# Six token blocks through the weights a quarter at a time, a weight conversion without GpSimd, a mask on ScalarE, and issue in the written order

## The chip, the cores and the metric

The kernel runs on one core of a Trainium2 chip. The metric is the device time of one execution in microseconds. Times are medians of several runs where several were made; "span" is the same execution in the trace, some 1.8 us shorter. "Cold" and "warm" are used of TensorE by the length of its matmuls: the same twelve h matmuls take 2.75 to 2.86 us when warm and up to 4.5 when cold.

## The reference, cut to what matters

```python
# r, k, v: (4 batches, 8 heads, 768 steps, 48 channels), f32
for t in range(S):
    cur = einsum('bhd,bhe->bhde', u * k[:, :, t], v[:, :, t])
    y[:, :, t] = einsum('bhd,bhde->bhe', r[:, :, t], state + cur)
    state = w * state + einsum('bhd,bhe->bhde', k[:, :, t], v[:, :, t])
x = y.transpose(0, 2, 1, 3).reshape(3072, 384)
h = x @ w_in                # 384 x 2048
g = h - tanh(h)
out = g @ w_out             # 2048 x 384
```

Two kinds of work: the recurrence, done in "units" of 64 steps and two batches (24 units), and the dense part, done in 12 blocks of 256 tokens with 8 dense steps each (96 steps). Two units make the input of one block. The weights arrive as 64-bit numbers and are turned into f32 on the chip.

## The kernel before

Engine names in the code: T is TensorE, V VectorE, A ScalarE, G GpSimd. A dense step is 12 h matmuls, then elementwise work on ScalarE, GpSimd and VectorE that makes g, and the output matmuls two steps later:

```python
        def first(f):
            h = ps_d.tile([128, 2, d.NT], F32, name="h", tag="h")
            ...                                    # 12 matmuls
            A.activation(s, hf, AF.Square)
            A.activation(th, hf, AF.Tanh)
            A.activation(q1, s, AF.Square, bias=m1b)
            A.activation(q2, s, AF.Square, bias=m2b)
            G.tensor_scalar(small, s, SMALL, None, ALU.is_lt)
            V.scalar_tensor_tensor(cube, s, C4, hf, ALU.mult, ALU.mult)
            V.tensor_tensor(gf, hf, th, ALU.subtract)
            V.scalar_tensor_tensor(cube, q1, K1, cube, ALU.add, ALU.mult)
            V.scalar_tensor_tensor(cube, q2, K2, cube, ALU.add, ALU.mult)
            V.copy_predicated(gf, small.bitcast(I32), cube)
            return g
```

A unit is one long chain through all engines:

```python
        G.tensor_tensor(kw[:, :, :D], kt, w_down, ALU.mult)
        ...
        for src in (rt, kw):
            for p in range(NP):
                T.transpose(turned[...], src[...], ident)
            if src is rt:
                V.tensor_tensor(halves(rT), turned, halves(w_up), ALU.mult)
            else:
                A.copy(halves(kT), turned)
        G.tensor_tensor(rk, rt[:, :, :D], kt, ALU.mult)
        G.tensor_tensor(rk, rk, ub, ALU.mult)
        yield
        V.tensor_reduce(du, rk, axis=mybir.AxisListType.X, op=ALU.add)
        G.tensor_tensor(at, same[...], du[...], ALU.mult)
        ...                                        # state x rT; rT x kT into lev
        yield
        V.copy_predicated(at, before, lev)
        yield
        ...                                        # at x vt; vt x kw: the "value groups"
        A.copy(xt[...], y_ps[...]); A.copy(rest, ...)
        yield
        V.tensor_tensor(now, kv_ps, now, ALU.add)  # the state
        G.tensor_tensor(now, now, w_all, ALU.mult)
        yield
```

In words: rT and kT are r and k turned round, kw is k times its decay, du is the share of the step itself, and `at` is first a mask (`same` times du: one GpSimd operation here, in the changed kernel's early units eight on ScalarE), into which the predicated copy then puts the product of rT and kT. The "value groups" use `at`. Note that `turned` is one buffer: the kw transposes may go only after rT has read the rt transposes. Units and dense steps are generators, and `weave` writes them into the program in turns. All 28 weight pieces are converted in the first two blocks' units, ahead of the first dense step. The framework's scheduler then chooses the order of the instructions on each engine; only the small matmuls are held to the written order:

```python
    def put(*args, **how):
        tc.keep_in_program_order(T.matmul(*args, skip_group_check=True, **how))
```

## Time and profile before

| | before |
|---|---|
| time, median of 4 runs | 728.44 us (726.28 to 729.8) |
| TensorE busy | 620.9 us, 86% |
| VectorE / ScalarE / GpSimd busy | 492.4 / 279.5 / 352.6 us |
| granted TensorE clock, mean | 0.946 |
| TensorE's time before 182 us beyond its work at the warm pace | 114.5 us, worked out in the prediction |
| of it without any matmul, by the trace's busy time | 93.1 us (182 less 88.9) |

Its lines stand in the prediction. Read them as one story: TensorE is full from a quarter of the way on, and the only time to win lies in the front, where the weights are converted.

### The profile page before, as it was taken

The numbers are of one execution on the slowest core, as the hardware profiler recorded it, in microseconds if no ns is written. First come the engines' busy times: TensorE is split into PE (matmuls) and PEld (weight loads), VectorE is DVE, ScalarE is ACT, GpSimd is POOL, SyncE is SP. The second block draws the span as 40 slices with busy tenths as digits, with TensorE's granted clock in tenths as the row PEclk, the third lists the DMA queues.
The fourth block names the chain that finished last, engine by engine and source line by source line (L and its number), as shares of the span: only waits on it lengthen the run. The fifth ranks groups of instructions, "written<-read, shape, count | busy, mean of one in ns | idle before, by whom it ended". The sixth has DMA issues, their size and how long they took to land.

```text
span 724.0 us, 13305 instructions
## 1 busy us (share of the span) xinstructions
PE 620.9 (86%) x5060; PEld 453.2 (63%) x5060; DVE 492.4 (68%) x739; ACT 279.5 (39%) x510; POOL 352.6 (49%) x289
## 2 busy tenths in 40 slices
PE   1462473657999999999999999999999999999996
PEld 0351452435776777777677777767777777777773
DVE  7764788989875664864865766748648656576563
ACT  1110413223443543444444434435435444354442
POOL 4775876758654543634545445436345243133231
PEclk9997586767999999999999999999999999999999
DMA  9457243422210211202102102112120010000001
GB/s 145 99 127 138 68 101 90 108 80 74 51 36 11 55 29 41 41 15 58 26 13 58 36 10 58 30 31 42 24 47 15 1 27 3 4 23 1 23 1 27
DMA packets 89722, 33.80 MB, mean 47 GB/s; under 512 B 80561, under 2 KB 86066, under 8 KB 89650
## 3 DMA queue, kind: packets, MB, share of 16 engines
q1 hardware_dynamic: 85042, 20.28, 14.9%
q10 hardware_dynamic: 4608, 12.59, 6.3%
q8 instruction: 42, 0.69, 0.4%
q14 instruction: 30, 0.25, 0.1%
HBM read 26.94 MB, written 4.72 MB: 44 GB/s over the span
## 4 chain that ended last, share of the span: by engine, by line
PE 68%; DVE 12%; DMA 8%; POOL 6%; issue 4%; SPq 1%; ACT 0%; ACTq 0%; DVEq 0%; POOLq 0%
PE o L177 33%; PE h L151 27%; PE yk_ps L348 4%; DMA st<-in_moe_w_out_dram 4%; DMA rt<-in_r_dram 3%; POOL part L119 3%; PE x_ps L363 2%; POOL rk L370 2%; POOL rk L371 2%; DVE st L116 1%; DVE part L114 1%; DVE w_in_sb L117 1%; DVE part L118 1%; DVE w_in_sb L115 1%; DVE cube L170 1%
## 5 line engine op out<-in xcount | busy, mean ns | idle before, releaser
L151 PE MATMUL h<-xt,w_in_sb 128*128 128x256 f32 x1152 | 276.4, 389 | 20.6 <-POOL w_in_sb L120 20.5
L177 PE MATMUL o<-w_out_sb,g 128*128 128x384 f32 x768 | 270.0, 498 | 11.8 <-DVE g L171 11.8
L166 POOL TENSOR_SCALAR small<-s 128x512 f32<-128x512 f32 x96 | 146.1, 1523 | 258.0 <-ACT s L162 249.7
L151 PEld LDWEIGHTS h<-xt,w_in_sb 128*128 128x128 f32 x1152 | 217.1, 194 | 59.8 <-POOL w_in_sb L120 22.9
L177 PEld LDWEIGHTS o<-w_out_sb,g 128*128 128x128 f32 x768 | 146.8, 194 | 102.4 <-issue 11.6
L167 DVE SCALAR_TENSOR_TENSOR cube<-s,h 128x512 f32<-128x512 f32 x96 | 65.7, 685 | 122.6 <-ACT th L163 122.4
L162 ACT ACTIVATE s<-h 128x512 f32<-128x512 f32 x96 | 57.3, 597 | 190.7 <-PE h L151 87.1
L170 DVE SCALAR_TENSOR_TENSOR cube<-q,cube 128x512 f32<-128x512 f32 x96 | 79.2, 825 | 7.6
L171 DVE COPY_PREDICATED g<-small,cube 128x512 f32<-128x512 int32 x96 | 78.5, 818 | 5.6
L169 DVE SCALAR_TENSOR_TENSOR cube<-q,cube 128x512 f32<-128x512 f32 x96 | 74.8, 779 | 0.0
L164 ACT ACTIVATE q<-s,m1b 128x512 f32<-128x512 f32 x96 | 69.3, 722 | 9.9 <-POOL part L119 9.9
L165 ACT ACTIVATE q<-s,m2b 128x512 f32<-128x512 f32 x96 | 69.0, 719 | 0.0
L168 DVE TENSOR_TENSOR g<-h,th 128x512 f32<-128x512 f32 x96 | 65.5, 682 | 0.0
L163 ACT ACTIVATE th<-h 128x512 f32<-128x512 f32 x96 | 56.8, 592 | 2.7 <-POOL part L119 2.7
L119 POOL TENSOR_TENSOR part<-part,st 128x384 f32<-128x384 f32 (+1 forms) x28 | 35.9, 1280 | 39.6 <-DVE part L118 22.8
L348 PE MATMUL yk_ps<-rT,state 48*64 48x64 f32 x704 | 27.7, 234 | 24.3 <-DVE state L416 19.3
L113 ACT ACTIVATE st<-st 128x384 f32<-128x384 uint32 (+1 forms) x28 | 17.1, 610 | 73.3 <-POOL part L119 34.5
L348 PEld LDWEIGHTS yk_ps<-rT,state 48*64 48x64 f32 x704 | 24.6, 146 | 33.1 <-issue 28.2
L376 POOL TENSOR_TENSOR at<-same,du 128x512 f32<-128x512 f32 x24 | 30.9, 1286 | 23.9 <-PE yk_ps L348 21.4
L365 DVE TENSOR_TENSOR rT<-x_ps,w_up 128x512 f32<-128x512 f32 x24 | 16.4, 685 | 29.3 <-PE x_ps L363 29.3
L374 DVE TENSOR_REDUCE du<-rk 128x8 f32<-128x384 f32 x24 | 13.2, 550 | 33.3 <-POOL rk L371 33.3
L370 POOL TENSOR_TENSOR rk<-rt,kt 128x384 f32<-128x384 f32 x24 | 26.6, 1109 | 16.5 <-DMA rt<-in_r_dram 9.5
(71 smaller groups left out, 459.8 us busy)
## 6 DMA issues: line engine op xcount, KB each, us to landing
st<-in_moe_w_out_dram ACTq DMA_DIRECT2D x16, 384.0 KB, 3.0
st<-in_moe_w_in_dram ACTq DMA_DIRECT2D x24, 192.0 KB, 3.3
rt<-in_r_dram SPq DMA_DIRECT2D x48, 96.0 KB, 3.1
kt<-in_k_dram SPq DMA_DIRECT2D x48, 96.0 KB, 3.0
vt<-in_v_dram SPq DMA_DIRECT2D x48, 96.0 KB, 2.8
out_dram<-o SPq DMA_DIRECT2D x48, 96.0 KB, 2.2
xt<-rest SPq DMA_DIRECT2D x144, 8.0 KB, 1.8
st<-in_moe_w_in_dram ACTq DMA_DIRECT2D x24, 64.0 KB, 3.3
```

The costliest lines, as they stand in the source:

```text
L119: G.tensor_tensor(part_f, part_f, lo_f, ALU.mult)
L151: T.matmul(h[:, z], w_in_sb[:, kk, (f + z) * 128 : (f + z + 1) * 128], xt[:, kk].rearrange("p b t -> p (b t)"), start=kk == 0, stop=kk == ...
L164: A.activation(q1, s, AF.Square, bias=m1b)
L165: A.activation(q2, s, AF.Square, bias=m2b)
L166: G.tensor_scalar(small, s, SMALL, None, ALU.is_lt)
L167: V.scalar_tensor_tensor(cube, s, C4, hf, ALU.mult, ALU.mult)
L168: V.tensor_tensor(gf, hf, th, ALU.subtract)
L169: V.scalar_tensor_tensor(cube, q1, K1, cube, ALU.add, ALU.mult)
L170: V.scalar_tensor_tensor(cube, q2, K2, cube, ALU.add, ALU.mult)
L171: V.copy_predicated(gf, small.bitcast(I32), cube)
L177: T.matmul(outs[i], g[:, z, i * C : (i + 1) * C], w_out_sb[:, f + z, :], start=f + z == 0, stop=f + z == d.NF - 1)
L348: tc.keep_in_program_order(T.matmul(*args, skip_group_check=True, **how))
```

## The change

Its intent is to fill that front. The weights come in eight pieces of 1536 columns; six blocks run their first quarter of the dense part as soon as the first quarter of the weights is there, then all six their second, and so on, with partial sums in SBUF. The conversion uses VectorE and ScalarE only, the mask `small` goes from GpSimd to ScalarE, early units use VectorE and ScalarE instead of GpSimd, and the scheduler is switched off, so that each engine issues in the written order. The diff, cut to its core:

```diff
-            G.tensor_tensor(part_f, part_f, lo_f, ALU.mult)
-            G.tensor_tensor(dst, dst, part_f, ALU.add)
...
+        V.tensor_scalar(power, hi, 0x7FF00000, None, ALU.bitwise_and)
+        A.activation(power, power, AF.Relu, scale=8.0, bias=self.bias)
+        V.tensor_scalar(bits, hi, 0xFFFFF, 0x100000, ALU.bitwise_and, ALU.bitwise_or)
+        A.activation(lo_f, lo, AF.Copy, scale=2.0**-52)
+        yield
+        V.scalar_tensor_tensor(dst, bits, 2.0**-20, lo_f, ALU.mult, ALU.add)
+        V.scalar_tensor_tensor(power, hi, 0x80000000, power, ALU.bitwise_and, ALU.bitwise_or)
+        yield
+        V.tensor_tensor(dst, dst, power.bitcast(F32), ALU.mult)
...
-            G.tensor_scalar(small, s, SMALL, None, ALU.is_lt)
+        A.activation(small, s, AF.Relu, bias=smallb, scale=-1.0)
...
+            if begun:
+                V.tensor_tensor(o, outs[i], o, ALU.add)      # partial sums
...
+        weave(blocks([0, 1]), pieces([0, 1]))
+        for q in range(4):
+            fs = (q * part, (q + 1) * part)
+            streams = [(chain.from_iterable(dense(j, xts[j], fs) for j in js), FIRST * part // 2)]
+            if q == 0:
+                streams.append(blocks(range(2, FIRST + 2)))
+            if q < 3:
+                streams.append(pieces([2 * q + 2, 2 * q + 3]))
+            weave(*streams)
...
+        early = n < L * (FIRST + 2)
+        E = V if early else G
+        E.tensor_tensor(kw[:, :, :D], kt, w_down, ALU.mult)
...
+        for h in range(H if early else 0):
+            A.mul(at[:, h % 2, h // 2], same, du[:, h : h + 1])
...
-        tc.keep_in_program_order(T.matmul(*args, skip_group_check=True, **how))
+        T.matmul(*args, skip_group_check=True, **how)
...
-        near(tc, r, k, v, w, u, out, shared, weights)
+        with tc.manual_schedule():
+            near(tc, r, k, v, w, u, out, shared, weights)
```

## The prediction

> **What bounds the kernel now.** I read the page first (busy shares, slices), then the table of stretches, then the costliest groups, then the timeline of one undisturbed step.
>
> ```profile
> span 724.0 us, 13305 instructions
> ...
> PE 620.9 (86%) x5060; PEld 453.2 (63%) x5060; DVE 492.4 (68%) x739; ACT 279.5 (39%) x510; POOL 352.6 (49%) x289
> ...
> PE   1462473657999999999999999999999999999996
> ...
> DVE  7764788989875664864865766748648656576563
> ...
> PEclk9997586767999999999999999999999999999999
> ```
>
> TensorE is full from slice 11 on. Before that it is half idle, and VectorE is busiest.
>
> ```profile
> 0.00:45.00 45.00, 13.71 (x220) 10.49 (x220) 33.67 (x60) 8.15 (x15) 31.13 (x43) 1.00 0.67 121
> 45.00:90.00 45.00, 19.89 (x298) 16.99 (x299) 26.87 (x46) 8.96 (x17) 31.46 (x28) 0.70 0.49 107
> ...
> 135.00:182.00 47.00, 26.42 (x197) 17.29 (x196) 42.42 (x61) 12.65 (x23) 33.03 (x26) 0.75 0.33 89
> ...
> 232.00:282.00 50.00, 49.39 (x433) 36.22 (x432) 32.66 (x48) 21.86 (x40) 23.14 (x19) 1.00 0.17 35
> ...
> 633.00:675.00 42.00, 41.95 (x162) 30.42 (x161) 26.44 (x40) 19.69 (x35) 12.29 (x8) 1.00 0.04 10
> ```
>
> The columns are the stretch, its length, then busy time of PE, PEld, DVE, ACT, POOL, granted clock, DMA share, GB/s. In the chain of waits the blocks stand 50.3 us apart from 182 us on while two attention units run beside each (nine blocks), and 41.7 us apart for the last two: TensorE alone sets the pace. So a unit costs TensorE (50.3 - 41.7) / 2 = 4.3 us, and all its work is 12 x 41.7 + 24 x 4.3 = 604 us. The other 120 us are idle: 7 after the last matmul, and 182 - (41.7 + 6 x 4.3) = 114.5 before 182 us, where the conversion of the weights passes 28 pieces through two staging buffers. That front is what the change attacks.
>
> ```profile
> L151 PE MATMUL h<-xt,w_in_sb 128*128 128x256 f32 x1152 | 276.4, 389 | 20.6 <-POOL w_in_sb L120 20.5
> ...
> L164 ACT ACTIVATE q<-s,m1b 128x512 f32<-128x512 f32 x96 | 69.3, 722 | 9.9 <-POOL part L119 9.9
> ```
>
> The matmuls that wait, wait for the conversion's last GpSimd step. The dense step I use as a ruler:
>
> ```profile
> 644.12 2.75 PE L151 MATMUL h<-xt,w_in_sb 128*128 128x256 f32 x12
> ...
> 646.97 0.60 ACT L162 ACTIVATE s<-h 128x512 f32<-128x512 f32 x1 [2.93 <-issue]
> 647.46 0.59 ACT L163 ACTIVATE th<-h 128x512 f32<-128x512 f32 x1
> ...
> 648.08 0.69 DVE L167 SCALAR_TENSOR_TENSOR cube<-s,h 128x512 f32<-128x512 f32 x1 [0.44 <-ACT th L163]
> 648.69 0.68 DVE L168 TENSOR_TENSOR g<-h,th 128x512 f32<-128x512 f32 x1
> ...
> 649.29 0.68 DVE L169 SCALAR_TENSOR_TENSOR cube<-q,cube 128x512 f32<-128x512 f32 x1
> ...
> 650.07 0.69 DVE L170 SCALAR_TENSOR_TENSOR cube<-q,cube 128x512 f32<-128x512 f32 x1
> ...
> 650.87 0.75 DVE L171 COPY_PREDICATED g<-small,cube 128x512 f32<-128x512 int32 x1
> ```
>
> TensorE goes on 2.6 us after it started h; VectorE starts 1.4 us after that and needs 3.5 us: g is ready about 5 us after h.
>
> **What the Trainium skill says.** "TensorE: Matmul & The Clock Gate", section "Architectural detail": ScalarE and VectorE are strict FIFO, and TensorE pulls only weight loads ahead. No trace line of before contradicts it; it means that a written order is an executed order, and a blocked instruction holds all behind it. The same page, Part 1: an idle window of about 3.4 us halves the clock until a busy one has passed. The trace agrees: after an idle 6.4 us at 144.9 four output matmuls took 2.90 us, against 2.74 for eight when warm. "ScalarE: Activation LUTs", "What ACT_TABLE_LOAD costs": an activation takes 186 ns + 0.833 ns an element, 93 more for each pointer operand, and neighbours overlap by 93. For 512 elements with one pointer that is 706 ns; the trace has 722. "GPSIMD Engine Reference", table of specifications: its SBUF port is shared with VectorE's two-input and two-port operations. The trace agrees: the conversion's fused two-input step took 1.37 to 1.65 us beside GpSimd (107.1, 112.0) and 0.69 alone (108.9).
>
> **The change, part by part.**
>
> Conversion. Uncontended, VectorE's one-input step takes 0.34 us for 384 columns and 0.43 for 512, the fused one 0.55 and 0.69, ScalarE's 0.56 and 0.67. Extended to 1536 columns: 1.15, 1.8 and 1.55 us. A new piece is 2 x 1.15 + 2 x 1.8 + 1.7 = 7.6 us on VectorE and 3.1 on ScalarE; eight are 61 and 25 us, against 98.9 of VectorE and 68.7 of GpSimd before. Real, and mostly hidden after the first quarter.
>
> Start: four units with two pieces, no dense work. The decay table is ready near 12 us as before. One unit in written order is kw, rT, transposes, kT, rk twice, du, eight ScalarE masks, predicated copy, two matmul groups, state: about 8 us, plus 15 us of conversion of which half stands on the path: 12 + 32 + 8 = 52 us, of which TensorE works 17.
>
> First quarter: twelve dense steps with twelve units. The instruction order shows exactly one unit between two h groups, and on VectorE the next unit's kw behind the dense chain. So every step is one loop, us by start-to-start: matmul end to VectorE start 1.4; five dense operations 3.6 (one more dependent pair than before); state 0.45, kw 0.4, rT 0.6, rk 0.5 and 0.6, du 0.6 (rows of 384 and 512 elements: 0.54, 0.685, 0.55); eight masks on ScalarE, with one pointer 0.24 each by the page, 1.9; wait and predicated copy 0.8; attention value groups 1.1 (64 matmuls at 227.9); h 2.6. Sum 14.6. The transposes and kT lie beside rk and du. Two pieces add 15 us in twelve steps, so 15.9 a step, 191 us; some cold stretches, say 4: 195 us. TensorE has only 12 x (5.2 + 4.3) = 114 us of work there.
>
> Quarters two to four: 18 blocks' quarters of two dense steps. TensorE wants 10.4 us each. But the single-buffered sums are now emptied by two VectorE adds behind the second dense chain, 5.0 + 0.9 after h, while TensorE returns after 5.2: 0.7 lost each. With conversion bursts: 18 x 11.4 = 205 us, against 187.
>
> Steady blocks, four left with units. Written order puts rT behind the dense chain and the state add, ready about 6.1 us after h; GpSimd's state multiply (0.89) and then kw (1.0 to 1.35) come behind that, 7.5 us. TensorE stands at the kw transposes 3.1 us after h (2.6 of output matmuls, 0.45 of rt transposes) and waits 4.4. Before, the scheduler put h matmuls there. First and last units about 3: 6 x 4.4 + 2 x 3 = 32 us, and idle over 3.4 us makes the next matmuls cold, 5: 4 x 50.3 + 37 = 238 us.
>
> Last two blocks 83, tail 7. The mask on ScalarE frees 146 us of GpSimd but is not on the path: ScalarE goes to 2.9 us a step of 5.2.
>
> Sum: 52 + 195 + 205 + 238 + 83 + 7 = 780 us.
>
> **Rivals.** (a) The intended one: quarters fill the front. Then only TensorE's work counts: 604 + 35 idle at the start + 7 = 646, perhaps 670 with small waits. For it: the front's 114 us of idle are real. Against it: one unit per dense step in a fixed order is a loop of 14.6 us whatever the engines' load is. (b) Front cured no further than now, but no stalls in the steady blocks: 52 + 190 + 195 + 201 + 90 = 728, the same. For it: the steady state is at 1.00 clock and full; against it: the in-order wait for rT and kw is in the order itself. (c) The clock falls in the first quarter as it did from 45 to 182 us (0.70 to 0.75): h, value groups and transposes stretch, 2 us more a step, 805 us. (d) VectorE becomes the bound in the middle quarters: 3.6 + 0.45 + 1.3 = 5.3 us a step against 5.2: no more than a few us.
>
> **Range and chances.** I take 775, a little under the sum because waits that I counted apart may cover one another. With every term at its kindest (45, 180, 192, 222, 90) it is 729; with (c) and 12 us more elsewhere 815. Range 730 to 812. Faster by over 2% needs a first quarter under some 150 us or no stalls at all: 0.12. Same: 0.14. Slower: 0.74.
>
> **What would show it.** In the changed profile: dense steps about 15 to 16 us apart in the first quarter, with TensorE near 60% busy there and the clock below 1; VectorE's h-to-g chain and the masks inside the loop; pairs of 10.4 to 11.5 us in the middle; blocks of about 59 us with units, waits of 3 to 5 us at the kw transposes released by GpSimd's kw or VectorE's rT; GpSimd near 15% busy. It is wrong if steps in the first quarter come 11 us apart or closer, if the middle runs above 12 us a pair, or if the steady blocks stay at 50 us.

## The result, and the profile after

| | before | after |
|---|---|---|
| time, median | 728.44 us (726.28 to 729.8, 4 runs) | 859.54 us (856.49 to 863.83, 4 runs) |
| ratio | | 1.181 (1.1745 to 1.1869) |
| TensorE busy | 620.9 us | 665.7 us |
| granted clock, mean | 0.946 | 0.899 |

A ratio is the mean time of one kernel's runs over the mean of the other's of the same rounds, so not quite the ratio of the medians. The change makes the kernel 131 us slower, where the prediction said 47. The page of the profile, in the same rows as before:

```profile
span 862.1 us, 12870 instructions
...
PE 665.7 (77%) x5062; PEld 495.3 (57%) x5062; DVE 495.5 (57%) x721; ACT 374.4 (43%) x722; POOL 64.8 (8%) x73
...
PE   0444657656645698989889998897797798899996
...
PEclk9999767686667789999999999999999999999999
```

TensorE is at 0.7 or less up to slice 14 (302 us), where before it was so up to slice 10 (181 us), and its clock is at 0.6 to 0.8 for eleven slices, where before had seven of 0.5 to 0.8. Behind that it no longer holds 9s. The table of stretches, cut at the borders of the change's parts (columns as in the prediction):

```profile
0.00:80.00 80.00, 25.39 (x484) 20.86 (x484) 35.35 (x59) 20.40 (x50) 8.40 (x23) 1.00 0.61 111
80.00:311.00 231.00, 145.94 (x1853) 117.55 (x1854) 99.92 (x150) 79.76 (x201) 16.70 (x12) 0.70 0.25 47
311.00:523.00 212.00, 195.34 (x721) 137.77 (x721) 170.95 (x234) 117.57 (x193) 5.93 (x4) 0.98 0.13 30
523.00:762.00 239.00, 205.61 (x1652) 151.66 (x1650) 127.97 (x192) 104.12 (x188) 33.76 (x35) 0.95 0.13 25
```

These are the start, the first quarter, quarters two to four, and the four blocks with units. In the first quarter no engine is near full: TensorE 63%, VectorE 43%, ScalarE 35%, GpSimd 7%. That is the sign of a loop of dependent instructions, not of a full engine. The waits view (who waits on whom, us in total, times and the longest) names the largest wait of TensorE, of which twelve waits and 60.0 us lie in the first quarter:

```profile
PE x_ps L414 <- DVE rT L416: 85.4, 18, 11.1
```

TensorE stands at the kw transposes until VectorE has made rT, and in the written order rT comes behind the whole elementwise chain of the step.

A step of the first quarter with no conversion in it, cut to the lines of the loop:

```profile
127.66 4.52 PE L165 MATMUL h<-xt,w_in_sb 128*128 128x256 f32 x12
...
133.33 0.69 DVE L182 TENSOR_TENSOR g<-h,th 128x512 f32<-128x512 f32 x1 [7.61 <-ACT th L178]
...
137.06 0.55 DVE L473 TENSOR_TENSOR state<-yk_ps,state 128x384 f32<-128x384 f32 x1
...
140.40 2.02 ACT L428 ACTIVATE at<-same,du 128x64 f32<-128x64 f32 x8
...
143.52 1.13 PE L396 MATMUL yk_ps<-at,vt 64*64 64x64 f32 x32 [0.93 <-DVE at L444]
144.43 1.05 PE L396 MATMUL yk_ps<-vt,kw 64*64 64x48 f32 x32
145.41 0.93 PEld L165 LDWEIGHTS h<-xt,w_in_sb 128*128 128x128 f32 x3
```

The prediction's links in their order: h, the dense chain on VectorE, the state, eight masks on ScalarE, the value groups, the next h 17.75 us after the last. The h group takes 4.52 us here, and took 2.75 in the ruler of before. The start holds two rows of weight loads that the prediction has no counterpart for:

```profile
0.80 17.16 ACTq L125 DMA_DIRECT2D st<-in_moe_w_in_dram  x8
...
21.59 0.56 DVE L410 TENSOR_TENSOR kw<-kt,w_down 128x384 f32<-128x384 f32 x1 [8.21 <-ACT w_down L339]
...
23.53 1.12 PE L414 MATMUL x_ps<-ident,kw 128*128 128x128 f32 x4 [0.78 <-DVE rT L416]
...
52.19 10.05 ACTq L125 DMA_DIRECT2D st<-in_moe_w_in_dram  x7
...
62.28 1.57 ACT L142 ACTIVATE power<-power,p_bias 128x1536 uint32<-128x1536 uint32 x1 [9.93 <-DMA st<-in_moe_w_in_dram]
...
65.91 0.56 DVE L473 TENSOR_TENSOR state<-yk_ps,state 128x384 f32<-128x384 f32 x1 [10.80 <-ACT rest L463]
```

ACTq is ScalarE's own sequencer. A row takes several issues together: a single one takes 0.3 to 0.5 us, but the eight lie over 17.16 us and the seven over 10.05, with gaps of up to 6 us between them; what holds the sequencer in the gaps the trace does not name. Until the last is out ScalarE's next instruction, written behind them, stands; behind it stand the copies that a unit needs, and behind those VectorE's state. One trap for the reader: the granted clock is given as 1.00 for the first 80 us, yet the kw transposes at 23.53 took 1.12 us, as long as the cold ones in the first quarter (1.11 at 138.72), where warm ones take 0.66 (e12, below). Judge the clock by the length of a known group.

In the blocks with units the prediction's wait is there to the digit, in the first line of these two from the waits view:

```profile
PE x_ps L414 <- POOL kw L410: 26.4, 6, 4.4
...
PE o L195 <- DVE part L203: 17.0, 17, 3.1
```

The second line is TensorE waiting for the sums to be emptied, nearly all of it in quarters two to four (16.7 us in 16); the prediction had 0.7 us eighteen times. The first wait in time order, with the cold h group that follows it:

```profile
559.82 0.99 POOL L410 TENSOR_TENSOR kw<-kt,w_down 128x384 f32<-128x384 f32 x1
560.87 0.91 PE L414 MATMUL x_ps<-ident,kw 128*128 128x128 f32 x4 [4.40 <-POOL kw L410]
561.57 4.23 PE L165 MATMUL h<-xt,w_in_sb 128*128 128x256 f32 x12
```

### The profile page after: what moved, and what is told of

Its sections match the earlier page's. It is cut to its first block, busy times and chain, and to the rows that moved or that the text cites. A ratio compares the mean times of both kernels' runs of the same rounds, so it can differ in the third digit from the quotient of the medians.

```text
span 862.1 us, 12870 instructions
## 1 busy us (share of the span) xinstructions
PE 665.7 (77%) x5062; PEld 495.3 (57%) x5062; DVE 495.5 (57%) x721; ACT 374.4 (43%) x722; POOL 64.8 (8%) x73
## 4 chain that ended last, share of the span: by engine, by line
PE 55%; DVE 23%; ACT 8%; issue 6%; DMA 4%; SPq 1%; POOL 1%; DVEq 0%; ACTq 0%; POOLq 0%
PE h L165 25%; PE o L195 18%; PE yk_ps L396 7%; DVE th L185 3%; DVE th L184 3%; DVE g L182 3%; DVE th L183 3%; PE x_ps L414 3%; ACT s L177 2%; DVE g L186 2%; ACT th L178 2%; PE x_ps L396 2%; DMA vt<-in_v_dram 2%; ACT st L144 1%; DVE part L203 1%
## 5 line engine op out<-in xcount | busy, mean ns | idle before, releaser
L165 PEld LDWEIGHTS h<-xt,w_in_sb 128*128 128x128 f32 x1152 | 234.2, 206 | 49.9 <-issue 0.8
L414 PE MATMUL x_ps<-ident,kw 128*128 128x128 f32 x96 | 24.6, 406 | 111.8 <-DVE rT L416 85.4
L186 DVE COPY_PREDICATED g<-small,th 128x512 f32<-128x512 int32 x96 | 71.7, 747 | 10.6 <-DVE th L185 0.9
L185 DVE SCALAR_TENSOR_TENSOR th<-q,th 128x512 f32<-128x512 f32 x96 | 67.0, 698 | 10.3 <-DVE th L184 0.5
L184 DVE SCALAR_TENSOR_TENSOR th<-q,th 128x512 f32<-128x512 f32 x96 | 66.7, 695 | 10.0
L181 ACT ACTIVATE small<-s,smallb 128x512 f32<-128x512 f32 x96 | 68.8, 716 | 0.0
L183 DVE SCALAR_TENSOR_TENSOR th<-s,h 128x512 f32<-128x512 f32 x96 | 65.9, 687 | 3.3
L476 POOL TENSOR_TENSOR state<-state,power 128x384 f32<-128x384 f32 x22 | 29.6, 1347 | 395.8 <-DVE state L473 355.0
L444 DVE COPY_PREDICATED at<-before,x_ps 128x512 f32<-128x512 int32 x24 | 17.3, 721 | 48.5 <-ACT at L428 24.4
L396 PE MATMUL yk_ps<-at,vt 64*64 64x64 f32 x768 | 23.7, 286 | 25.1 <-DVE at L444 18.6
L396 PEld LDWEIGHTS yk_ps<-at,vt 64*64 64x64 f32 x768 | 19.6, 190 | 32.4 <-DVE at L444 21.3
```

The source lines that it names most:

```text
L165: T.matmul(h[:, z], w_in_sb[:, kk, (f + z) * 128 : (f + z + 1) * 128], xt[:, kk].rearrange("p b t -> p (b t)"), start=kk == 0, stop=kk == ...
```

## The experiments

I cut every trace at the same five places, the start of the tanh in dense steps 1, 12, 48, 80 and 96, read from ScalarE's timeline. The stretches add to the span. In e5 and e11 the tanh is written one step later, which moves their cuts by some us. The expectations cut one step later, at 13, 49 and 81, which gives 221, 219 and 236 us for the changed kernel's quarter, middle and blocks with units. The traced run of the changed kernel was the longest of its four (863.83 us), so differences of under 5 us in this table carry nothing, and differences to it add up to some 4 us more than those of the medians.

| | to step 1 | to 12 | to 48 | to 80 | to 96 | to the end | span |
|---|---|---|---|---|---|---|---|
| after | 94.8 | 216.0 | 212.1 | 242.4 | 82.7 | 14.0 | 862.1 |
| e1 scheduler back | 72.2 | 117.7 | 188.1 | 195.7 | 82.7 | 14.5 | 671.0 |
| e3 loads on GpSimd | 84.7 | 205.5 | 214.6 | 243.3 | 82.7 | 15.0 | 845.9 |
| e4 filler in one gap | 98.7 | 205.4 | 212.1 | 242.4 | 82.7 | 13.6 | 855.0 |
| e5 elementwise a step late | 100.9 | 163.3 | 206.8 | 211.1 | 82.2 | 15.5 | 779.7 |
| e9 filler in two gaps | 98.4 | 209.2 | 213.2 | 243.9 | 82.7 | 13.5 | 860.9 |
| e10 kw a step late | 93.9 | 216.1 | 212.1 | 196.8 | 82.7 | 13.5 | 815.2 |
| e11 e3 + e5 + e10 | 92.0 | 155.9 | 203.7 | 196.2 | 82.1 | 16.2 | 746.1 |
| e12 filler, trimmed | 97.4 | 201.4 | 212.1 | 241.2 | 82.7 | 13.6 | 848.5 |

**Is it the order, or the quarters and the new conversion?** Everything of the change but the order:

```diff
-        with tc.manual_schedule():
+        if True:
             near(tc, r, k, v, w, u, out, shared, weights)
-        T.matmul(*args, skip_group_check=True, **how)
+        tc.keep_in_program_order(T.matmul(*args, skip_group_check=True, **how))
```

> The changed kernel with one part undone: the scheduler chooses the order again, everything else (quarters, new conversion, mask on ScalarE, early work on VectorE) stays. Theory (the fixed order is the loss: one loop per dense step in the first quarter, waits at the kw transposes later): first quarter about 140 us instead of 231, blocks with units back near 50 us instead of 61, about 700 to 735 us in all. Rival (the quarters, the sums on VectorE and the conversion on two engines are themselves the loss): still over 820 us.

Measured: 673.88 us (672.07 to 675.3), 0.927 of before (0.9236 to 0.9302): better than the theory's range. The page:

```profile
span 671.0 us, 12904 instructions
...
PE 603.7 (90%) x5062; PEld 444.8 (66%) x5062; DVE 491.7 (73%) x721; ACT 373.7 (56%) x722; POOL 61.2 (9%) x73
...
PE   0147889898899999999999999999999999999995
...
PEclk9998799999999999999999999999999999999998
```

TensorE is at 0.8 or more from slice 5 on: the front is filled as the change meant it. Out of the same instructions, written order costs 186 us: in the table 22.6 in the start, 98.3 in the first quarter, 24.0 in the middle, 46.7 in the blocks with units (191 us between the two traced runs).

The mirror of it, the kernel before with its scheduler taken away:

```diff
-        tc.keep_in_program_order(T.matmul(*args, skip_group_check=True, **how))
+        T.matmul(*args, skip_group_check=True, **how)
...
-        near(tc, r, k, v, w, u, out, shared, weights)
+        with tc.manual_schedule():
+            near(tc, r, k, v, w, u, out, shared, weights)
```

> The kernel before with one part of the change alone: it issues in the written order. Theory: the nine blocks with units go from 50.3 to about 58 to 60 us because TensorE waits at the kw transposes, and the front gets no shorter: 790 to 850 us. Rival (order does not matter by itself, only together with the quarters): 720 to 745 us.

Measured: 856.2 us in one look, beside 726.88 for before. So written order costs the kernel before 129 us too, a little above the theory's range and far from the rival's. But it does so in another way than in the changed kernel, and only half of it as the theory said: blocks with units came at 55 to 58 us instead of 50.3, which makes 67 us from dense step 12 to 80 by the table's cuts, while the front up to step 12 grew by 63 (265.0 against 202.5). There all 28 conversions stand in the text ahead of the first dense step, whose tanh comes at 194.9 us instead of 76.8, with TensorE busy for 32 us until then. With both kernels in written order, the rest of the change is worth nothing (856 against 860); with both scheduled, it is worth 53 us.

**What of the change is worth the 53 us, under the scheduler?** Three runs, each one edit on e1, on one chip against the same runs of before (e1 was timed on another chip, against 726.88 us for before there and 726.4 here):

```diff
-FIRST = 6
+FIRST = 1
```

> The scheduler's order with one block instead of six passing the weights quarter by quarter; new conversion, mask and early work stay. If the quarters give the gain of the scheduled version over the kernel before: 705 to 730 us. If the cheaper conversion and the relieved GpSimd give most of it: 675 to 695 us.

Measured: 692.31 us, 0.953 of before (0.951 to 0.9544). The second reading holds: only one block in quarters keeps 34 of the 53 us. The quarters of the other five blocks give 18, and the rest comes from what is left of the change: the conversion in eight larger pieces without GpSimd, with one block in quarters, and early units on VectorE and ScalarE. I did not split those.

```diff
-        A.activation(small, s, AF.Relu, bias=smallb, scale=-1.0)
+        nc.gpsimd.tensor_scalar(small, s, SMALL, None, ALU.is_lt)
```

> The scheduler's order and all of the change, but the mask of small values back on GpSimd. If the mask is off the path, as I predicted: within 8 us of the scheduled version's 674. If GpSimd's port or its 1.5 us a step mattered: 685 us or more.

Measured: 680.66 us, 0.935 of before (0.9314 to 0.9389): some 7 us slower than e1, within the reading that the mask matters little, though a real loss of 1% is not excluded. Freeing an engine that is not the bound is worth nearly nothing, as the prediction said of this mask.

```diff
-            self.nc.scalar.dma_start(out=dst[to, kk], in_=src)
+            self.nc.gpsimd.dma_start(out=dst[to, kk], in_=src)
```

> The scheduler's order and all of the change, with the weight loads issued from GpSimd. Theory (ScalarE stands[...] until about 21 us in the scheduled version too): 8 to 15 us less, 659 to 666 us. Rival (the scheduler already fills that time): 670 to 676 us.

Measured: 679.72 us, 0.935 (0.9338 to 0.9371): a miss for both readings, slightly slower. It is not that the scheduler had put other ScalarE work ahead of the issues: in e1's trace eight of them lie from 0.80 to 19.10 us, and the copy of w_down comes behind, at 22.70. With the issues moved that copy comes at 20.76, but the start gains only 0.6 us (71.6 against 72.2), and the first quarter takes 125.7 us instead of 117.7. Why, I did not find out. All three came out slower than e1, e7 and e8 by some 1%, and across chips; e1 is the fastest version and beats both kernels.

**What do ScalarE's load issues cost in written order?** The same edit as e8, made on the changed kernel.

> The changed kernel with the weight loads issued from GpSimd instead of ScalarE. Theory (three times ScalarE stands[...]: until 21 us, from 50 to 62 us, and near 218 to 245 us): 25 to 35 us less, 825 to 835 us, and the decay table copied near 14 us. Rival (the data themselves come late, whoever asks): within 8 us of 860.

Measured: 847.72 us in one look, between the two, so a miss for both. The start and the first quarter lose 10 us each by the table, and the rest, 2.5 us and less the other way, carries nothing; that makes 16 us between the traces and 12 by the medians. The start kept more than the theory hoped. The first stall had a second cause beneath it:

```profile
20.33 0.56 DVE L410 TENSOR_TENSOR kw<-kt,w_down 128x384 f32<-128x384 f32 x1 [11.46 <-DMA kt<-in_k_dram]
```

With w_down no longer late, the first kw waits 11.46 us for kt, whose transfer lands only 1.3 us sooner than the kw started before (20.33 against 21.59). kt had been issued by 5.32 us, and its median time to land is 3.1 us over the run, so for this load the rival, data that come late, holds. So nearly all of the 17.16 us of issue in front was hidden behind a load; the 10.05 us at 52 and the 9.56 us at 234 were not.

**Is the first quarter slow because TensorE is cold?** In the step shown above h (4.52 us) and the value groups (1.13) took some 1.6 times as long as when warm (2.86 and 0.69). Twenty-four more rt transposes, which nobody needs, fill the first gap:

```diff
-            for p in range(NP):
+            for p in list(range(NP)) * (7 if src is rt and early and n >= 2 * L else 1):
```

> The changed kernel with the rt transposes of the twelve early units written seven times over (same values, same place), so that TensorE is busy while it waits for rT. Theory (part of the missed 36 us of the first quarter is the half clock): h groups there fall from about 4.2 to 2.6 us, value groups from 2.0 to 1.1, steps from 17.5 to 15 us, 25 to 35 us less in all: 825 to 835 us. Rival (the loop is longer for another reason): step stays at 17 us or more, 855 to 890 us.

Measured: 856.78 us in one look, and h was still cold: a miss, though the first quarter came down from 216.0 to 205.4 us. The filler ended the first gap only, and in some steps not even that. There is a second, in front of the value groups, where TensorE waits for the masks:

```profile
184.88 0.69 PE L396 MATMUL yk_ps<-at,vt 64*64 64x64 f32 x32 [2.30 <-DVE at L444]
185.39 0.70 PE L396 MATMUL yk_ps<-vt,kw 64*64 64x48 f32 x32
186.03 4.42 PE L165 MATMUL h<-xt,w_in_sb 128*128 128x256 f32 x12
```

The value groups are warm (0.69 against 1.13), but after 2.30 us of idleness the h group behind them is not. So fill both gaps:

```diff
+            for p in list(range(NP)) * (9 if src is rt and early and n >= 2 * L else 1):
...
                     put(lev[HALF[z], i, p], kT[HEAD[i], p, z], rT[HEAD[i], p, z], start=True, stop=True)
+        for p in list(range(NP)) * (5 if early and n >= 2 * L else 0):
+            T.transpose(turned[...], rt[...], ident)
```

> The changed kernel, written order kept, with idle-filling transposes on TensorE in the first twelve steps: the rt transposes 9 times over (36 instead of 4, ahead of the wait for the kw transposes) and 20 more behind the rT x kT group (ahead of the wait for the mask). Run e4 filled the first gap only, and its h groups stayed cold (3.9 to 4.5 us) after the 2.3 us wait for the mask. Theory, that a half-speed TensorE is the larger part of what the prediction missed in the first quarter: with both gaps filled the h groups fall to 2.6 to 2.9 us, the steps without conversion to 14 to 15 us, the granted clock there above 0.9, the first quarter from 221 to 185 to 197 us, total 828 to 840. Rival, that the clock is a by-product and the loop is set by VectorE, ScalarE and the loads: steps stay at 16.5 or more, first quarter 208 or more, total 850 or more.

Measured: 862.78 us in one look, though every h group was warm at 2.86 us. Plain steps came at 16.7 us. That looks like the rival, but two waits in the trace are the fillers' own:

```profile
142.24 0.69 DVE L416 TENSOR_TENSOR rT<-x_ps,w_up 128x512 f32<-128x512 f32 x1 [0.62 <-PE x_ps L414]
...
147.63 0.72 DVE L446 COPY_PREDICATED at<-before,x_ps 128x512 f32<-128x512 int32 x1 [3.05 <-PE x_ps L444]
```

rT waits for the last filler, and so does the mask's predicated copy, whose masks were done at 146.63. The experiment paid on the path what it saved on the path. So I trimmed the fillers to end just before they are in the way:

```diff
-            for p in list(range(NP)) * (9 if src is rt and early and n >= 2 * L else 1):
+            for p in list(range(NP)) * (7 if src is rt and early and n >= 2 * L else 1):
...
-        for p in list(range(NP)) * (5 if early and n >= 2 * L else 0):
+        for p in list(range(NP)) * (3 if early and n >= 2 * L else 0):
```

> As e9, with fewer fillers: rt transposes 7 times over (28) and 12 more behind the rT x kT group. In e9 every h group was warm (2.86 us) and the plain step still took 16.7, but the fillers themselves were in the way twice: rT waited 0.6 us for the last of 36, and the mask's predicated copy, which was free to go about 0.9 us sooner, waited for the last of 20. Theory: the half-speed TensorE costs about 2 us a step (h 4.3 against 2.9, value groups 2.0 against 1.2), so without the fillers' own 1.5 us the plain steps come at 15.0 to 15.5 us; first quarter 200 to 208; total 845 to 852. Rival, that the clock is no term of the loop at all: 16.5 or more though h is warm. Either way the first quarter stays far above 160: what is left is the chain on VectorE and ScalarE and the load stalls.

Measured: 850.39 us in one look, first quarter 206.5 us by the expectation's cut (201.4 by the table's), plain steps 15.0 to 15.1 us but for the first of them: the theory on all counts. The loop, in the same lines as for the changed kernel:

```profile
130.62 2.86 PE L165 MATMUL h<-xt,w_in_sb 128*128 128x256 f32 x12
...
134.63 0.69 DVE L182 TENSOR_TENSOR g<-h,th 128x512 f32<-128x512 f32 x1 [5.14 <-ACT th L178]
...
138.39 0.54 DVE L475 TENSOR_TENSOR state<-yk_ps,state 128x384 f32<-128x384 f32 x1
...
141.73 2.02 ACT L428 ACTIVATE at<-same,du 128x64 f32<-128x64 f32 x8 [0.40 <-DVE du L425]
...
144.59 0.69 PE L396 MATMUL yk_ps<-at,vt 64*64 64x64 f32 x32 [0.89 <-DVE at L446]
145.11 0.63 PE L396 MATMUL yk_ps<-vt,kw 64*64 64x48 f32 x32
145.67 2.86 PE L165 MATMUL h<-xt,w_in_sb 128*128 128x256 f32 x12
```

It lets the loop be taken apart link by link, each from one start to the next:

| link | predicted | after | e12, warm |
|---|---|---|---|
| h to the first VectorE step | 4.0 | 5.67 | 4.01 |
| five dense steps on VectorE | 3.6 | 3.73 | 3.76 |
| state, kw, rT, rk, rk, du | 3.15 | 3.34 | 3.34 |
| masks, wait, predicated copy | 2.7 | 3.12 | 2.86 |
| value groups | 1.1 | 1.89 | 1.08 |
| sum | 14.55 | 17.75 | 15.05 |

The warm step is 2.7 us shorter, and 2.5 of them lie in the two links that TensorE has in the loop. The cold TensorE is a consequence of the loop's gaps that then lengthens the loop. Over the stretch it is worth less than 2.7 us a step: the six plain steps got shorter by 11.3 us together, the five with conversion by 3.4.

**Is the loop itself the cost?** Write the elementwise work of a dense step one step after its matmuls, so that the unit's small VectorE steps no longer queue behind a chain that waits for h:

```diff
-            waiting.append((j, fs, f, first(xt, f)))
+            held.append((j, fs, f, matmuls(xt, f)))
+            if len(held) > 1:
+                jj, ffs, ff, h = held.pop(0)
+                waiting.append((jj, ffs, ff, rest(h)))
```

> The changed kernel, still in the written order, but the text writes the elementwise work of a dense step one step after its matmuls, so that no VectorE or ScalarE instruction of a unit stands behind work that waits for the newest h. Theory (the loop through h, the dense chain and the next unit is the loss, not the writing itself): steps of the first quarter fall from 17 to 21 us to 11 to 14, blocks with units from 59 to 50 to 53, the middle loses its waits; 720 to 770 us. Rival (single engines or the clock are the bound whatever the order): 830 us or more.

Measured: 781.43 us in one look, beside 726.4 for before. 78 us come back without a scheduler, 11 short of the theory's range. The table shows 53 in the first quarter and 31 in the blocks with units, and some 5 each way elsewhere.

**Is the wait for kw alone what the blocks with units lose?** One move, for the late units only: the kw transposes and the kT copy go behind the next dense step.

```diff
-        for src in (rt, kw):
-            ...                        # transposes, then rT or kT
+        turn(rt)
+        if early:
+            turn(kw)
         ...
         yield
+        if not early:
+            turn(kw)
```

> The changed kernel, written order kept, with one move for the 8 units of the steady blocks only: their kw transposes and the kT copy are written behind the next h and output group instead of right behind the rt transposes. Theory, that the steady blocks lose their 8 us a block only because TensorE stands in the written order in front of kw, which GpSimd brings late: the wait of 4.4 us goes, the 32 steady steps fall from 236 to 203 to 212 us (12 us pairs), the rest stays, total 825 to 838. Rival, that the wait moves to the next link (kT copy, rT x kT group, mask, value group, all in the same order): the steady steps stay at 224 or more, total 847 or more.

Measured: 817.02 us in one look. The stretch fell from 242.4 to 196.8 us (236 to 196 by the expectation's cut), further than the theory's range, and level with the scheduler's 195.7. No other stretch moved. The move takes away 45.6 us, not only the 26.4 of the waits listed: with them go two waits for rT, 6.7 us, and the cold h groups behind the six waits (4.23 against 2.86 us in the lines above, so some 8 us by estimate); some 4 us stay unassigned.

**Do the repairs add?** e5, e3 and e10 in one kernel.

> Written order kept, the three repairs together: the elementwise work of a dense step written one step after its matmuls (as e5), the weight loads issued from GpSimd (as e3), the steady kw transposes a step later (as e10). Theory, that the loss is made of these separate waits, which add: e5 gave 78 us, e3 12, e10 should give about 20 more: 740 to 758 us. Rival, that the repairs cover the same time (deferring already takes most of the kw wait and of the load stalls): 762 to 782 us. Either way it stays above the 674 us of the scheduler's order if order as a whole, and not one wait, is what the scheduler repairs.

Measured: 747.85 us in one look, the theory's range. The three alone give 78, 12 and 43 us, 133 in all; together 112, since e5 had already taken 31 us of the stretch that e10 mends. What is left in written order:

```profile
92.00:256.00 164.00, 120.88 (x1586) 95.54 (x1585) 97.65 (x141) 77.24 (x186) 22.82 (x20) 0.81 0.31 56
256.00:460.00 204.00, 190.98 (x740) 137.21 (x740) 171.23 (x236) 116.60 (x191) 8.25 (x12) 0.99 0.13 30
460.00:652.00 192.00, 192.00 (x1642) 144.08 (x1637) 134.32 (x190) 103.27 (x191) 36.17 (x35) 1.00 0.14 29
```

against the scheduler's first quarter:

```profile
72.00:195.00 123.00, 109.62 (x1850) 81.14 (x1851) 99.16 (x151) 83.20 (x202) 22.94 (x22) 0.97 0.56 104
```

With the late units mended TensorE is full there (192.00 of 192.00, clock 1.00). The first quarter is still 38 us longer than the scheduler's in the table, at a clock of 0.81. Another 20 lie in the start and 16 in the middle. Those 74 us I have not split into single waits.

## Why the prediction was right or wrong

It was right in direction and in two of its mechanisms, the loop of the first quarter and the wait for kw, and wrong in size: 775 us with a range to 812, against 859.5. Two of its steps failed. The first quarter was summed with a warm TensorE (14.6 us a step) and 15 us of conversion, and came to 17.2 and 26.9. The start was put at 52 us, with a path on which neither ScalarE's load issues nor a late kt stood, and took 80.8. By its own terms, measured in the trace of the changed kernel:

| term | predicted | measured | how measured |
|---|---|---|---|
| start | 52 | 80.8 | the fifth unit's kw starts at 80.80 |
| first quarter | 195 | 230.1 | from there to the tanh of step 12, 310.9 |
| quarters two to four | 205 | 212.1 | to the tanh of step 48 |
| four blocks with units | 238 | 242.4 | to the tanh of step 80 |
| last two blocks and tail | 90 | 96.7 | to the end of the span |
| sum | 780 | 862.1 | |

- **The wait at the kw transposes** was right: predicted 4.4 us, six times; the waits view has 26.4 us in 6. e10 shows that it and what hangs on it are the whole loss of that stretch. The last three terms together came out 18 us over, on 533.
- **The first quarter** failed in its base step, 14.6 us. The step's links were right for a warm TensorE: e12 measured 15.05. But TensorE was cold in that loop, and plain steps came at 17.2 on average (six of them, 16.8 to 17.6): 2.6 us on eleven steps is 29, less the 4 us that the sum allowed for "some cold stretches". That all of it is the cold is not shown: e12 took back 15. The prediction had this as rival (c), "2 us more a step", and made it a branch of its own, though its page of before already showed 0.70 to 0.75 for a TensorE 44 to 56% busy; and of the 114.5 us that it called idle in that front, only 93 are without a matmul, which leaves 21 to matmuls longer than the warm ones it reckoned with. In this loop TensorE stood idle for over a third of the time, 3.5 us at one stretch in the step shown, and the cold step was the usual one.
- **Conversion in the first quarter** was put at 15 us. The five longer steps exceed 17.2 by 3.1, 3.7, 2.8, 13.7 and 3.6, 26.9 us. 10.8 of it are one stall: that step took 30.9 us, and 20.1 in e3, where ScalarE does not issue the load. This and the base step are 37 us over; the first and incomplete step of the stretch, 14.0 us to its tanh, and rounding bring it to 35.
- **The start** was 29 us over. 9.6 are the first kw at 21.6 instead of 12, where both ScalarE's issues and the kt transfer are late (e3: 20.3 with the issues gone). 9.9 are the second stall behind ScalarE's loads. The last 9 are sizing: four units and two pieces took 59.2 us from the first kw to the fifth, 49.3 without the stall, against 40. Either more than the assumed half of the conversion stood on the path, or the units, whose matmuls were cold here too, took longer than 8 us; I did not split that.
- **ScalarE as a DMA issuer** was not in the prediction at all. It said that a blocked instruction holds all behind it, and did not apply that to the loads written in front of ScalarE's own work.
- **The rivals**: (a), the filled front at 646 to 670, is what the change does once the scheduler is back (674); (b) did not come; (c) came; (d), VectorE as the bound in the middle, is not what the runs show: e1 does the same middle in 188.1 us. Of the 7 us over the prediction's 205 there, 4 are the wait for the sums (16.7 us against 18 times 0.7).
- **The signs** that it named: steps of 15 to 16 us (17.2 came), TensorE near 60% busy (63%), middle pairs of 10.4 to 11.5 us (11.8), blocks of about 59 us with units (60.6), GpSimd near 15% busy (8%).

So the loss against the same text under the scheduler is settled as one of order (e1), and its largest single parts are known, each by one look: the kw wait with its cold h groups (43 us by e10), the elementwise chain in front of the units' steps (78 us by e5, which covers part of the former), the cold TensorE in the first quarter (up to 2.7 us a step, 15 us of the stretch by e12), the load issues (12 us by e3). They overlap, and 74 us of what is left with three repairs stay unsplit.

## What to carry to other kernels

When a change also fixes the order of issue, judge the order first: follow one step from its first matmul to the next and ask of every engine what is written in front of the instruction that matters, DMA issues included. The loop here, in which no engine was busy over two thirds, was a chain, and its TensorE ran cold; for such a loop reckon with the cold durations as well, which the stalled stretches of the profile before already show. And when a filler or a repair changes nothing, look for its own wait before believing the rival: e9 and e12 differ only in 16 filler transposes for each unit.

## What the Trainium skill lacked or had wrong

- "TensorE: Matmul & The Clock Gate", Part 1, puts the idle window that halves the clock at about 3.4 us. Here a shorter gap sufficed: after an idle 2.30 us in e4 an h group took 4.42 us, against 2.86 after 0.89 in e12. The page calls its window free-running, which may allow that; its section "A second HAM failure mode: psum-queue depth-cycling" tells of frequent short idle times that make the clock swing, but gives no length for them.
- "DMA: Bandwidth & Descriptors", section "Issuing engines are not separate DMA queues", says that the time to initiate a DMA on the sequencer "is usually small relative to the DMA itself". For a single issue the trace agrees: a median of 0.35 us, against 6.6 to 7.1 from issue to landing. But eight in a row lay over 17.16 us and seven over 10.05, and ScalarE's work stood behind them. No page that I read warns that loads issued from ScalarE hold up its compute in this way.
- No page gives a size for what issue in the written order costs a kernel with two interleaved chains: here 186 us of 860 (e1 against after) and 129 of 856 (e2 against before).
